# Joined PSUM pairs, whole float32 second products and half tiles in a gated attention plus feed-forward kernel

## The chip, the cores and the metric

One core of a Trainium2 chip (trn2) runs the kernel. The metric is the device time of one execution in microseconds (us). The kernel before took 519.96 us, the median of three runs (518.54 to 520.96).

## The reference

The input is four batches of eight heads, 768 tokens each, head size 48, all float32. The attention is a gated recurrence; its output is the input of a feed-forward layer (FF) with 2048 hidden units.

```python
f = 1.0 / (1.0 + np.exp(-f_logit))
for t in range(S):
    state = f[:, :, t, :, None] * state + einsum('bhd,bhde', k[:, :, t], v[:, :, t])
    y[:, :, t] = einsum('bhd,bhde->bhe', q[:, :, t], state)
x = y.transpose(0, 2, 1, 3).reshape(B * S, H * D)     # 3072 x 384
h = x @ w_in                                           # 384 x 2048
out = (h * np.clip(h + 3.0, 0.0, 6.0) / 6.0) @ w_out   # 2048 x 384
```

## The kernel before

**Attention.** The tokens are cut into chunks of 128 (six per batch), and a chunk of one batch with all its heads is a unit: 24 units, 0 to 23, with the batches of one chunk next to each other. For a unit, VectorE scans the gates backward (`back`, L313), inverts the end values (`rend`, L329 and L330), scans forward (`fwd`, L333), and multiplies keys and queries by the scans (`kmul` L326, `qmul` L339, on VectorE or GpSimd). TensorE transposes the keys (`tk` L400, copied by ScalarE at L407), forms the new state from keys and values (`kv` L419), the scores within the chunk (`att` L378), the part from the carried state (`qs` L451) and the part from the masked scores (`av` L465). The results leave PSUM, TensorE's accumulator memory of eight banks, like this: scores by two masking multiplications, one per bank (`mask0`, `mask1`, L388); states by pairs of additions (`carry0` L432, `carry1` L440, or copies on ScalarE in the first chunk); the output y as a rounded high part on ScalarE (`xh0`, `xh1` L496, `y3h` L482) and the rest on VectorE (`xl0`, `xl1` L502, `y3l` L485). Two DMAs then move rows into the gaps of the FF input (`hole` L508).

**Weights.** The weights arrive as 64-bit words, one tile of 128 hidden units at a time (`ld` L228). ScalarE and VectorE turn each tile into float32 and split it into a high and a low part (L234 to L271; `low` L271 is the last step). There are 16 tiles.

**FF.** Four units make a group of 512 tokens; six groups by 16 hidden tiles give 96 FF tiles. A tile is a first product (`mm1` L528, nine matmuls of 128x512: high by high, high by low, low by high, over three parts of the input), the activation (`relu` L538 on ScalarE, `g` L542 on VectorE), a split of its result (`gh` L547 on ScalarE, `gl` L551 on VectorE), and a second product (`mm2` L565, nine matmuls again, since both sides come in two parts). In the last group a third of the second product runs in halves of 256 tokens (L577).

**Order.** The order of every step is written out in the list ORDER; ON_POOL names the steps that run on GpSimd. Each engine runs its own steps in that order. The digits behind a TensorE step name its PSUM banks. `warm` steps are matmuls on zeros (L660) that fill waits at the start. All loads and stores are issued by SyncE (SP), in order.

```python
P3 = ((0, 0), (0, 1), (1, 0))        # mm1: first index the weight's part, second the input's
a, b = P3[-i]                        # mm2: high by high, low weight by high, high weight by low
```

## Time and profile before

| what | value |
|---|---|
| median of 3 runs | 519.96 us |
| span of the profiled execution, first to last instruction | 519.0 us |
| TensorE matmuls busy | 499.7 us, 96% |
| VectorE busy | 316.3 us, 61% |
| ScalarE busy | 215.5 us, 42% |
| GpSimd busy | 55.5 us, 11% |
| mean granted TensorE clock | 0.987 of full speed |
| bytes moved by DMA | 41.97 MB |

The profile is one execution taken by the hardware profiler; its times count from the span's start. PE is TensorE's matmul side and PEld its weight loads, DVE is VectorE, ACT ScalarE, POOL GpSimd, SP SyncE. A matmul's end is modelled, so the starts of successive groups are the better measure of its pace. The profiled execution took 519.0 us between its first and last instruction, 0.96 us less than the median of the runs.

### The profile page before, as it was taken

Reading aid. Unit: us, or ns where it says so; the run is one execution under the profiler, and the core shown is the slowest. Engines: PE = TensorE matmul, PEld = TensorE weight load, DVE = VectorE, ACT = ScalarE, POOL = GpSimd, SP = SyncE. Lnnn points to the kernel's source line nnn. Section 1 sums busy time; section 2 is a strip of 40 time slices with the busy share of each in tenths; the row PEclk is TensorE's granted clock in tenths of the full one; section 3 lists DMA queues with packets and bytes.
Section 4 is the critical chain, followed back from the end, with each engine's and each line's share of the span. In section 5 each row is a group of like instructions: output and inputs, shape, how many; then the busy total and the mean of one; then the engine's idle time right before and its main releaser. Section 6 shows DMA issues by size and latency. Waiting matters only on the chain.

```text
span 519.0 us, 11607 instructions
## 1 busy us (share of the span) xinstructions
PE 499.7 (96%) x4931; PEld 391.9 (76%) x4931; DVE 316.3 (61%) x599; ACT 215.5 (42%) x390; POOL 55.5 (11%) x61
## 2 busy tenths in 40 slices
...
GB/s 240 242 259 204 140 134 165 255 125 42 80 1 123 53 65 92 97 0 25 98 70 16 115 77 58 39 52 35 64 105 11 12 1 8 62 1 2 0 1 66
DMA packets 24554, 41.97 MB, mean 81 GB/s; under 512 B 2480, under 2 KB 17072, under 8 KB 24496
## 3 DMA queue, kind: packets, MB, share of 16 engines
...
q8 instruction: 41, 0.67, 0.6%
...
## 4 chain that ended last, share of the span: by engine, by line
PE 82%; DVE 8%; ACT 4%; issue 3%; DMA 1%; SPq 0%; POOL 0%; DVEq 0%; ACTq 0%; POOLq 0%
PE h L528 36%; PE o L565 33%; PE y L465 3%; PE o_half L577 2%; PE y L451 2%; PE at L378 2%; PE tk L400 2%; PE kv L419 2%; DVE raw L263 1%; DMA raw<-w 1%; PE idle L660 1%; ACT top L243 1%; ACT weight L268 1%; DVE gg L551 1%; DVE top L259 1%
## 5 line engine op out<-in xcount | busy, mean ns | idle before, releaser
L528 PE MATMUL h<-xt,weight 128*128 128x512 f32 x864 | 220.5, 401 | 2.2 <-ACT raw L234 1.2
L565 PE MATMUL o<-gg,weight 128*128 128x512 f32 x816 | 208.7, 399 | 0.3 <-ACT gg L547 0.3
L528 PEld LDWEIGHTS h<-xt,weight 128*128 128x128 f32 x864 | 160.8, 190 | 40.7 <-ACT top L243 1.3
L565 PEld LDWEIGHTS o<-gg,weight 128*128 128x128 f32 x816 | 151.4, 188 | 36.8 <-DVE gg L551 0.4
L542 DVE SCALAR_TENSOR_TENSOR tg<-tg,h 128x512 f32<-128x512 f32 x96 | 65.9, 686 | 123.7 <-ACT tg L538 123.3
L538 ACT ACTIVATE tg<-h,half 128x512 f32<-128x512 f32 x96 | 66.1, 688 | 178.7 <-PE h L528 176.9
L551 DVE TENSOR_TENSOR gg<-tg,gg 128x512 fp32r<-128x512 f32 x94 | 65.9, 701 | 40.9 <-ACT gg L547 36.9
L547 ACT ACTIVATE gg<-tg 128x512 fp32r<-128x512 f32 x96 | 60.6, 632 | 58.2 <-DVE tg L542 57.4
L326 POOL TENSOR_TENSOR qkf<-qkf,suffix 112x512 f32<-112x512 f32 x17 | 23.2, 1363 | 249.1 <-DVE tg L542 96.1
L313 DVE TENSOR_TENSOR_SCAN suffix<-gates,unit 112x516 f32<-112x516 f32 x24 | 30.3, 1261 | 3.0 <-ACT gates L307 2.8
L333 DVE TENSOR_TENSOR_SCAN suffix<-gates,rend 112x516 f32<-112x516 f32 x24 | 30.1, 1253 | 0.8 <-POOL qkf L326 0.5
L339 POOL TENSOR_TENSOR qkf<-qkf,suffix 112x512 f32<-112x512 f32 x15 | 18.0, 1202 | 42.9 <-DVE suffix L333 39.2
L388 DVE TENSOR_TENSOR a<-at,causal 128x256 f32<-128x256 f32 x48 | 18.1, 416 | 7.3 <-PE at L378 7.1
L465 PEld LDWEIGHTS y<-a,v 64*48 64x48 f32 (+1 forms) x768 | 13.4, 124 | 10.8 <-issue 6.2
L407 ACT ACTIVATE ktok<-tk 128x448 f32<-128x448 f32 (+1 forms) x24 | 12.3, 512 | 19.5 <-PE tk L400 19.4
L465 PE MATMUL y<-a,v 64*48 64x64 f32 (+1 forms) x768 | 17.5, 225 | 2.1 <-DVE a L388 2.0
L263 DVE SCALAR_TENSOR_TENSOR raw<-top,raw 128x768 int16<-128x768 int16 x16 | 18.2, 1138 | 0.5
L378 PE MATMUL at<-qkf 48*64 48x64 f32 x768 | 17.1, 227 | 1.4 <-ACT state L438 1.4
L660 PE MATMUL idle<-blank 128*128 128x512 bf16 x58 | 17.2, 445 | 1.1 <-DVE blank L198 1.1
L268 ACT ACTIVATE weight<-raw 128x768 fp32r<-128x768 f32 x16 | 13.5, 845 | 10.8 <-DVE raw L263 10.8
L496 ACT ACTIVATE xt<-y 112x128 fp32r<-112x128 f32 (+1 forms) x48 | 14.0, 327 | 9.1 <-PE y L465 9.1
L419 PE MATMUL kv<-v,ktok 64*48 64x48 f32 (+1 forms) x768 | 16.2, 216 | 1.6 <-ACT ktok L407 1.4
...
## 6 DMA issues: line engine op xcount, KB each, us to landing
...
gates<-fg SPq DMA_DIRECT2D x24, 226.2 KB, 2.9
...
```

The source lines that it names most:

```text
L263: nc.vector.scalar_tensor_tensor(upper, conv[f]["y"], 8.0, upper, op0=ALU.mult, op1=ALU.add)
L313: nc.vector.tensor_tensor_scan(flat(sf)[:, ::-1], gt[:, 1:][:, ::-1], flat(unit)[:, ::-1], 0.0, op0=ALU.mult, op1=ALU.add,)
L333: nc.vector.tensor_tensor_scan(flat(sf), gt[:, :NP * (C + 1)], flat(rend), 0.0, op0=ALU.mult, op1=ALU.add,)
L378: nc.tensor.matmul(d["ps"][e][HC * odd:HC * (odd + 1), 2 * n + c], t[rs, 1, n, c, odd], t[rs, 0, n, c, odd], start=True, stop=True,)
L419: nc.tensor.matmul(d["kv"][odd][r:r + m, c, n], d["ktok"][rs, 2 * n + part, r:r + m], heads_of(vt[rs], part, n, e)[:, :D], start=(odd, e) ...
L465: nc.tensor.matmul(d["y"][odd][to:to + m, n, cs], heads_of(vt[rs], c, n, e)[:, :m], d["a"][rs, 2 * n + c, e], start=False, stop=True, skip ...
L528: nc.tensor.matmul(h, win[:, f, a, k * 128:(k + 1) * 128], g["xt"][:, k, :g["n"] // C, b], start=i == 0, stop=i == 3 * KT - 1,)
L538: nc.scalar.activation(d["t"], d["h"], AF.Relu, bias=half, scale=1.0 / 6.0)
L542: nc.vector.scalar_tensor_tensor(d["t"], d["t"], 1.0, d["h"], op0=ALU.min, op1=ALU.mult)
L547: nc.scalar.activation(d["gg"][:, 0], d["t"], AF.Copy)
L551: engine("gl", f if g["name"] == "0" else NU).tensor_tensor(d["gg"][:, 1], d["t"], d["gg"][:, 0].bitcast(F32), op=ALU.subtract)
L565: nc.tensor.matmul(g["o"][m], wout[:, f, a, m * 128:(m + 1) * 128], g[f]["gg"][:, b], start=f == 0 and i == 0, stop=f == NF - 1 and i == 2 ...
```

## The change

1. PSUM is now held as two pairs of banks and one single bank. Scores, new states and outputs of a unit lie in one pair, and leave it in one instruction: one `mask`, one `carry0`, one `carry1`, one `xh`, one `xl`. The rows that `hole` moves become a fourth slab of the FF input. States and outputs of neighbouring units share a pair (outputs in columns 0 to 255 of each bank, states from 256 on). Ahead of `av`, TensorE waits on a semaphore until the matmuls of `qs` are done.
2. The second product of the first eight tiles is made of three whole float32 matmuls (`mm2x`, and `mm2a`, `mm2b` for halves). Those tiles need no `gh` and `gl`. A DMA (`wd`) copies the output half of the weight tile in whole float32 to the place of its low part; the low part is made there later (`lowo`), and that of the input half on its own (`lowi`).
3. The first five tiles run in halves of 256 tokens (`mm1a`, `relua`, `ga`, `mm2a` and the same with b), so that the first half needs units 0 and 1 only.
4. Raw weights have two buffers and not three, with two more for the float32 words.
5. ORDER and ON_POOL are new.

```diff
 ON_POOL = """
-kmul.1 qmul.1 kmul.3 qmul.3 kmul.4 qmul.4 kmul.5 gl.0 decay.5 low.3 kmul.6 decay.6 low.9 kmul.7 decay.7 qmul.7
...
+qmul.0 qmul.1 kmul.3 decay.4 qmul.5 kmul.6 decay.6 kmul.7 decay.7 qmul.9 qmul.10 decay.10 qmul.11 decay.11 qmul.12
...
+decay.19 qmul.20 decay.20 qmul.21 kmul.22 qmul.22 kmul.23 qmul.23 lowi.1 lowi.2 lowo.3 lowi.4 lowi.5 lowo.5 lowo.7
...
 ORDER = """
-load.0 loadq.0 load.1 loadv.0 loadq.1 loadv.2 loadv.1 gate.0 loadq.2 back.0 rend.0 kmul.0 gate.1 fwd.0 warm.13
...
+load.0 loadq.0 loadv.0 loadv.1 load.1 loadq.1 loadv.2 gate.0 ld.0 loadq.2 back.0 ld.1 rend.0 kmul.0 warm.16 tk.0.4
...
+    pairs = [ps_g.tile([128, 2, 512], F32, name=f"pair{i}") for i in range(2)]
+    single = ps_g.tile([128, 512], F32, name="single")
...
+    def conv_keep(f):
+        nc.sync.dma_start(out=weight[:, f, 1, OUTS].bitcast(F32), in_=conv[f]["w"][:, OUTS])
...
+        "low": lambda f: conv_low("low", f, slice(0, WN), conv[f]["w"]),
+        "lowi": lambda f: conv_low("lowi", f, INS, conv[f]["w"][:, INS]),
+        "lowo": lambda f: conv_low("lowo", f, OUTS, weight[:, f, 1, OUTS].bitcast(F32)),
...
-            d["ps"] = [bank([128, NP, HC], f"at{i}_{e}") for e in range(2)]
+            d["at"] = pair()[:, :, :NP * HC].rearrange("r e (p t) -> r e p t", t=HC)
...
+        def mask():
+            d["a"] = sb.tile([128, NP, 2, HC], F32, tag="a", name=f"a{i}")
+            nc.vector.tensor_tensor(
+                d["a"].rearrange("r p e t -> r e p t"), d["at"],
+                causal.unsqueeze(1).unsqueeze(1).broadcast_to([128, 2, NP, HC]), op=ALU.mult,
+            )
...
-            d["kv"] = [bank([128, 2, 2, D], f"kv{i}_{odd}") for odd in range(2)]
+            d["kv"] = pair()[:, :, 256:256 + 4 * D].rearrange("r o (c n d) -> r o c n d", c=2, n=2)
...
-            d["y"] = [bank([128, 2, C], f"y{i}_{odd}") for odd in range(2)]
+            d["y"] = pair()[:, :, :2 * C].rearrange("r o (n t) -> r o n t", t=C)
...
+            d["qs"] = nc.cur_bb.bb.instructions[-1]
...
         def av():
             vt = values[i]
+            hold = nc.tensor.nop()
+            after(hold.ins, d["qs"], mybir.DependencyClass.Sync)
...
+        def xh():
+            nc.scalar.activation(parts(0), d["y"][:PR], AF.Copy)
+        def xl():
+            nc.vector.tensor_tensor(parts(1), d["y"][:PR], parts(0).bitcast(F32), op=ALU.subtract)
...
+    def mm2_whole(g, f):
+        outs_of(g, f)
+        for m in range(KT):
+            nc.tensor.matmul(
+                g["o"][m], wout[:, f, 1, m * 128:(m + 1) * 128].bitcast(F32), g[f]["t"],
+                start=f == 0, stop=f == NF - 1, skip_group_check=True,
+            )
+    def half_of(p):
...
+        def mm2(g, f):
+            outs_of(g, f + p)
+            for m in range(KT):
+                nc.tensor.matmul(
+                    g["o"][m][:, p * 256:(p + 1) * 256],
+                    wout[:, f, 1, m * 128:(m + 1) * 128].bitcast(F32), g[f, p]["t"],
+                    start=f + p == 0, stop=False, skip_group_check=True,
+                )
```

How the order moves shows at three places. The names in the rows are the tiles written and read, with their unit or FF tile; L numbers are lines of the version that the rows belong to.

**VectorE at units 1 and 2, the first weight tile.** Before, the scores are masked and the outputs split by several instructions each, and the first weight tile (`raw0`, `top0`) comes behind unit 3's scans:

```order
L388 TENSOR_TENSOR a1_344<-at1_0_310,causal_80 128x4x64
L388 TENSOR_TENSOR a1_344<-at1_1_311,causal_80 128x4x64
L313 SCALAR_TENSOR_TENSOR suffix1_74<-gates1_73,unit_90 112x516
L329 TENSOR_SCALAR ends_111<-suffix1_74 112x4
L330 RECIPROCAL rend_109<-ends_111 112x4
L485 TENSOR_TENSOR y3_1_401<-y1_1_299,y3_1_401 112x128
L502 TENSOR_TENSOR xt0_248<-y1_1_299,xt0_248 112x128
L333 SCALAR_TENSOR_TENSOR suffix1_74<-gates1_73,rend_109 112x516
L247 TENSOR_SCALAR raw0_308<-top0_405 128x768
L502 TENSOR_TENSOR xt0_248<-y1_0_298,xt0_248 112x2x128
```

With the change, one instruction each does unit 1's mask and split, and the weight tile comes ahead of unit 2's scan:

```order
L240 TENSOR_SCALAR raw0_127<-top0_252 128x768
L392 TENSOR_TENSOR a1_305<-pair0_70,causal_83 128x2x4x64
L246 TENSOR_SCALAR top0_252<-top0_252 128x768
L252 TENSOR_TENSOR top0_252<-top0_252,raw0_127 128x768
L256 SCALAR_TENSOR_TENSOR w0_283<-top0_252,w0_283 128x768
L493 TENSOR_TENSOR xts_111<-pair1_71,xts_111 112x2x2x128
L320 SCALAR_TENSOR_TENSOR suffix0_75<-gates0_74,unit_93 112x516
```

The weight work moved ahead of two scans, and five instructions of unit 1 became two.

**TensorE behind unit 2, and SyncE's queue there.** Before, the first FF product stands behind unit 4's `av`. With the change the first half of tile 0 (`th0_0`, `single` of 256 columns) stands between unit 2's `qs` and `av`:

```order
L454 MATMUL pair0_70<-qkf2_129,middle0_96 64x64 x8
L575 MATMUL single_72<-xts_111,weight_73 128x256 x9
L471 MATMUL pair0_70<-a2_449,v2_124 64x64 x8
L471 MATMUL pair0_70<-a2_449,v2_124 48x64 x8
L404 MATMUL pair1_71<-ident_78,qkf3_215 128x112 x4
L593 MATMUL o0_0_482<-th0_0_454,weight_73 128x256
```

In SyncE's queue the copies of whole weights (`weight<-w0`, `weight<-w1`) stand between the loads:

```order
L310 DMA v4_338<-v 128x400
L498 DMA xts_111<-xts_111 16x3x256 x2
L272 DMA weight_73<-w0_283 128x384
L222 DMA raw2_351<-w 128x3072
L301 DMA gates0_74<-fg 112x517
L222 DMA raw3_428<-w 128x3072
L305 DMA qkf5_447<-qk 112x1024
L310 DMA v5_480<-v 128x400
L301 DMA gates1_76<-fg 112x517
```

Two units' work moved from ahead of the first FF product to behind it, and each copy is a step that the loads behind it are issued after.

**TensorE at units 14 and 15.** Before, the attention products stand in several stretches between FF products:

```order
L451 MATMUL y14_0_2984<-qkf14_2357,decayed2_104 64x64 x2
...
L378 MATMUL at14_1_3003<-qkf14_2357 64x64
L565 MATMUL o2_0_2590<-gg2_9_2967,weight_70 128x512
...
L528 MATMUL h2_11_3042<-xt2_1915,weight_70 128x512 x9
...
L400 MATMUL tk15_3071<-ident_75,qkf15_2870 128x112 x4
L528 MATMUL h2_12_3076<-xt2_1915,weight_70 128x512 x9
L465 MATMUL y14_0_2984<-a14_3034,v14_2425 48x64 x2
...
L419 MATMUL kv15_0_3110<-v15_2920,ktok15_3086 64x48
```

With the change `qs`, the next unit's `att`, `av` and the next unit's `kv` follow each other:

```order
L454 MATMUL pair0_70<-qkf14_2149,decayed0_98 64x64 x8
L454 MATMUL pair0_70<-qkf14_2149,middle0_96 64x64 x8
L385 MATMUL pair1_71<-qkf15_2452 64x64 x16
L471 MATMUL pair0_70<-a14_2574,v14_2181 48x64 x16
L423 MATMUL pair0_70<-v15_2489,ktok15_2633 64x48
...
L517 MATMUL single_72<-xts_111,weight_73 128x512 x9
```

Three stretches of attention work between FF products became one, and the transposes of units 15 and 16 stand together elsewhere.

## Rows read from the trace of the kernel before

**Rows 1.** Two stretches: us, busy us (count) of PE, PEld, DVE, ACT, POOL, clock, DMA.

```profile
91.00:104.00 13.00, 11.91 (x110) 8.87 (x108) 12.63 (x21) 8.04 (x11) 2.93 (x3) 1.00 0.77 254
460.00:500.00 40.00, 40.00 (x200) 33.44 (x199) 13.58 (x22) 11.90 (x18) 0.00 (x0) 1.00 0.00 1
```

**Rows 2.** The chain that ended last, in order of time: start us, us, what.

```profile
110.64 1.86 issue
112.50 0.78 PE tk L400 x4
113.28 3.46 PE h L528 x9
...
124.31 4.22 PE h L528 x18
128.53 2.10 PE o L565 x9
```

**Rows 3.** The same chain at its end.

```profile
510.60 2.15 PE o_half L577 x18
```

**Rows 4.** VectorE's timeline: start us, us, engine, line, operation, out and in.

```profile
124.58 0.96 DVE L271 TENSOR_TENSOR weight<-raw,weight 128x768 fp32r<-128x768 f32 x1
```

**Rows 5.** Groups of VectorE instructions: count, busy us, mean ns, idle before and its releasers.

```profile
L542 DVE SCALAR_TENSOR_TENSOR tg<-tg,h 128x512 f32<-128x512 f32 x96 | 65.9, 686 | 123.7 <-ACT tg L538 123.3
L551 DVE TENSOR_TENSOR gg<-tg,gg 128x512 fp32r<-128x512 f32 x94 | 65.9, 701 | 40.9 <-ACT gg L547 36.9 <-PE o_half L577 2.1 <-PE o L565 1.4
L388 DVE TENSOR_TENSOR a<-at,causal 128x256 f32<-128x256 f32 x48 | 18.1, 416 | 7.3 <-PE at L378 7.1
L502 DVE TENSOR_TENSOR xt<-y,xt 112x256 fp32r<-112x256 f32 x24 | 10.0, 418 | 0.0
L502 DVE TENSOR_TENSOR xt<-y,xt 112x128 fp32r<-112x128 f32 x24 | 6.9, 287 | 1.2 <-ACT y L482 0.8 <-ACT xt L496 0.3
L432 DVE TENSOR_TENSOR middle<-kv,decayed 112x96 f32<-112x96 f32 x40 | 8.3, 251 | 3.4 <-PE kv L419 3.3
L271 DVE TENSOR_TENSOR weight<-raw,weight 128x768 fp32r<-128x768 f32 x14 | 14.9, 1067 | 1.2 <-ACT weight L268 0.9
L313 DVE TENSOR_TENSOR_SCAN suffix<-gates,unit 112x516 f32<-112x516 f32 x24 | 30.3, 1261 | 3.0 <-ACT gates L307 2.8
L326 DVE TENSOR_TENSOR qkf<-qkf,suffix 112x512 f32<-112x512 f32 x7 | 5.3, 761 | 4.9 <-DMA qkf<-qk 4.8
```

**Rows 6.** TensorE's timeline at unit 2's carried-state product and at the first FF product.

```profile
28.45 0.58 PE L451 MATMUL y<-qkf,middle 48*64 48x64 f32 x14 [0.44 <-ACT middle L430]
...
43.63 1.19 PE L528 MATMUL h<-xt,weight 128*128 128x512 f32 x4
```

**Rows 7.** TensorE's timeline around units 8 to 10, between FF products.

```profile
154.85 0.60 PE L400 MATMUL tk<-ident,qkf 112*128 112x112 f32 x4
155.46 2.35 PE L528 MATMUL h<-xt,weight 128*128 128x512 f32 x9
157.74 0.67 PE L465 MATMUL y<-a,v 64*48 64x64 f32 x32
158.22 0.63 PE L419 MATMUL kv<-v,ktok 64*64 64x48 f32 x32
158.79 2.37 PE L565 MATMUL o<-gg,weight 128*128 128x512 f32 x9
161.00 0.55 PE L400 MATMUL tk<-ident,qkf 112*128 112x112 f32 x4
161.31 2.34 PE L528 MATMUL h<-xt,weight 128*128 128x512 f32 x9
163.59 0.46 PE L451 MATMUL y<-qkf,decayed 48*64 48x64 f32 x16
```

**Rows 8.** Weight loads of the FF products: count, busy us, mean ns, idle before.

```profile
L528 PEld LDWEIGHTS h<-xt,weight 128*128 128x128 f32 x864 | 160.8, 190 | 40.7 <-ACT top L243 1.3 <-ACT ktok L407 0.8 <-DVE a L388 0.6
```

**Rows 9.** A kind of DMA: count, KB each, median us from issue to landing.

```profile
gates<-fg SPq DMA_DIRECT2D x24, 226.2 KB, 2.9
```

More of the change, by code (lines that the diff above doesn't have):

```diff
@@ new lines @@
+wd.0 ld.2 high.0 mid.1 kmul.2 rend.2 warm.12 tk.2.4 lowi.0 gate.3 fwd.2 ktok.2 warm.2 kv.2.0 lim.1 load.4 qmul.2
+carry0.2 dif.1 att.2.2 carry1.2 back.3 ld.3 qs.2.0 mm1a.0.4 loadq.5 mask.2 kmul.3 rend.3 relua.0 av.2 ga.0 fwd.3
+tk.3.2 xh.2 loadv.5 mm2a.0 ktok.3 z.2 xl.2 load.5 qmul.3 kv.3.2 gate.4 hole.2 top.1 att.3.0 carry0.3 carry1.3 mask.3
+cy.2 wd.1 qs.3.2 loadq.6 back.4 av.3 high.1 loadv.6 xh.3 mid.2 kmul.4 xl.3 lowi.1 tk.4.4 mm1a.1.0 rend.4 hole.3 ktok.4
+lim.2 fwd.4 gate.5 kv.4.2 relua.1 z.3 dif.2 ga.1 decay.4 ld.4 load.6 mm2a.1 top.2 back.5 cy.3 wd.2 mm1b.0.4 high.2
@@ new lines @@
+mid.3 kmul.5 mm1b.1.1 relub.0 lim.3 gb.0 lowi.2 tk.5.0 rend.5 relub.1 mm2b.0 carry0.4 ktok.5 dif.3 decay.5 ld.5
+mm1a.2.4 gb.1 gate.6 fwd.5 z.4 mm1b.2.0 top.3 relua.2 mm2b.1 relub.2 ga.2 qmul.5 wd.3 cy.4 gb.2 load.7 carry1.4 mm2b.2
+high.3 mid.4 qmul.4 lim.4 mm2a.2 lowi.3 dif.4 z.5 back.6 mm1a.3.4 ld.6 gate.7 mm1b.3.1 top.4 relua.3 ga.3 kmul.6
+high.4 wd.4 att.4.2 rend.6 mm2a.3 mask.4 relub.3 cy.5 lowi.4 gb.3 mm1a.4.4 mid.5 fwd.6 mm2b.3 relua.4 lim.5 load.8 z.6
+ga.4 dif.5 tk.6.0 mm2a.4 qmul.6 ld.7 ktok.6 top.5 mm1b.4.4 back.7 cy.6 wd.5 qs.4.0 relub.4 mid.6 gate.8 gb.4 kv.5.2
@@ new lines @@
+decay.6 loadq.7 av.4 high.5 rend.7 lim.6 kv.6.0 loadv.7 carry0.5 lowi.5 mm1.5.4 carry0.6 carry1.5 xh.4 dif.6 carry1.6
+lowo.3 ld.8 z.7 xl.4 mm2b.4 relu.5 top.6 g.5 kmul.7 cy.7 wd.6 att.5.2 hole.4 att.6.0 mask.5 high.6 mm2x.5 mid.7 lowo.4
+lim.7 lowi.6 dif.7 fwd.7 ld.9 mm1.6.4 z.8 top.7 qmul.7 cy.8 wd.7 tk.7.2 load.9 lowo.0 ktok.7 mid.8 relu.6 lowo.1 lim.8
+high.7 g.6 qs.5.2 av.5 decay.7 kv.7.2 dif.8 mm2x.6 lowi.7 xh.5 ld.10 top.8 loadv.8 z.9 loadq.8 gate.9 xl.5 lowo.5 cy.9
+mask.6 hole.5 mm1.7.4 high.8 lowo.6 mid.9 carry0.7 lim.9 low.8 mm1.8.0 relu.7 dif.9 z.10 lowo.2 ld.11 top.9 relu.8 g.7
@@ new lines @@
+cy.10 carry1.7 mm2x.7 g.8 high.9 mid.10 back.8 gh.8 lim.10 gl.8 qs.6.0 att.7.2 dif.10 av.6 low.9 ld.12 mm2.8 xh.6
+loadv.9 top.10 loadq.9 z.11 mask.7 lowo.7 cy.11 xl.6 mm1.9.4 high.10 mid.11 hole.6 kmul.8 lim.11 low.10 mm1.10.2
+relu.9 dif.11 z.12 g.9 ld.13 top.11 gh.9 qs.7.0 relu.10 gl.9 av.7 cy.12 g.10 mm2.9 loadv.10 high.11 mid.12 loadq.10
+rend.8 gh.10 lim.12 low.11 xh.7 mm1.11.4 dif.12 gl.10 z.13 ld.14 top.12 mm2.10 relu.11 fwd.8 cy.13 g.11 load.10
+high.12 mid.13 tk.8.3 qmul.8 gh.11 ktok.8 lim.13 low.12 mm1.12.4 dif.13 z.14 gl.11 ld.15 mm2.11 gate.10 top.13 relu.12
@@ new lines @@
+tk.15.4 relu.36 tk.16.1 mm1.37.2 ktok.15 gl.35 ktok.16 g.36 gate.17 fwd.16 gh.36 mm2.35 relu.37 back.17 load.18 g.37
+mm1.38.4 rend.17 gh.37 gl.36 gl.37 gate.18 qmul.16 mm2.36 relu.38 back.18 g.38 mm2.37 gh.38 gl.38 mm2.38 mm1.39.4
+mm1.40.3 relu.39 g.39 gh.39 mm1.41.4 relu.40 gl.39 g.40 gh.40 mm2.39 relu.41 gl.40 g.41 gh.41 mm2.40 gl.41 mm2.41
+qs.14.0 att.15.2 decay.16 loadq.17 av.14 kv.15.0 mask.15 loadv.17 mm1.42.4 xh.14 xl.14 carry0.15 hole.14 carry1.15
+mm1.43.2 relu.42 kmul.17 g.42 gh.42 fwd.17 mm1.44.4 relu.43 gl.42 load.19 g.43 qmul.17 mm2.42 rend.18 gh.43 relu.44
```

346 lines of the change are left out of this document (149 added, 197 removed).

## The prediction, made before the changed kernel ran

> **What bounds the kernel now.** I read the tenths in 40 slices first, then busy times by stretch, then the chain of waits in order of time, and TensorE's and VectorE's timelines where the chain changes hands. Two stages are to be seen. In 91 to 104 us VectorE is busy 12.63 of 13 us; in 460 to 500 us TensorE is busy all 40 us [rows 1]. The chain shows where the first stage gives way: at 110.64 TensorE idles 1.86 us, then needs 3.46 us for nine matmuls of a first product that take 2.11 us later (4.22 for 18), and from there the chain is TensorE's alone [rows 2]. I cut the run at the end of FF tile 15's first product, the last that needs a new weight: 128.53 us [rows 2]. From there to the end of the last half product, 510.60 + 2.15 = 512.75 us [rows 3], are 384.2 us of TensorE; the rest of the span, 519.0 - 512.75 = 6.25 us, is the last copy, store and close. The sum is 128.53 + 384.22 + 6.25 = 519.0, the profiled execution; the median of the runs stands 0.96 us above.
>
> **Stage 1, VectorE.** The last weight part (`low.15`) starts at 124.58 and takes 0.96 us, so it ends at 125.54 [rows 4]; TensorE reached tile 15 some 3 us later, held up by the slow stretch at 110 to 117 us [rows 2]. I count VectorE's instructions up to `low.15` in both orders.
> Gone: 6 `g` at 0.686 and 6 `gl` at 0.701 (8.3 us); 16 masks at 18.1/48 = 0.377 (6.0); the three parts of `xl` for 8 units at 0.418 + 0.287 + 0.287 (7.9; the smallest, L485, has the 128-column shape); 8 pairs of carries at 2 x 8.3/40 = 0.415 (3.3); 6 whole `low` at 1.067 (6.4). Together 31.9 us [rows 5].
> Added: 10 half `g` of 256 columns, which I take at the mask's 0.42 (4.2); 9 masks of 512 columns and 8 `xl` of 512. No row has these, so they are bounded from below by 0.418 (256 columns) and from above by two such (0.84); the step from 128 to 256 columns costs 0.131, so 512 cost about 0.418 + 2 x 0.131 = 0.68, near the 0.686 of `g`, which reads as many from PSUM (17 x 0.67 = 11.4). 10 joined carries between 0.25 and 0.415, taken as 0.33 (3.3). 4 `lowi` and 5 `lowo` of half width, 1.067/2 = 0.53 (4.8). New on VectorE, since GpSimd has fewer of them: 4 `kmul` at 0.761 and 2 `qmul`, taken as the same (4.6). One more `back` and one more `fwd` at 1.26 (2.5), one `decay` at about 0.4. Together 31.2 us [rows 5].
> So VectorE's work up to `low.15` is 0.7 us less: the joins and the missing `gl` pay for what came over from GpSimd and for unit 8, which is now done earlier. I take VectorE's waits as they were, and `low.15` ends at 125.54 - 0.7 = 124.8. Only the last three of a first product's nine matmuls use the low weight, so tile 15 ends 0.7 us behind it: **125.5 us**, if TensorE is there. ScalarE (8.04 of 13 us busy) and GpSimd (2.93) have room in that stage [rows 1]: ScalarE loses six `gh` and two of three copies per unit, GpSimd has 16 steps up to the cut and not 18. The eight `wd` copies and what they hold up in SyncE's queue I cost at nothing, since the loads run ahead of their use; that cover is a rival below.
>
> **Stage 1, TensorE.** It must now do more: by the cut, one first product less (-2.1; tile 16 follows the cut), unit 8's `qs`, `att` and `av` more (about 0.5 + 0.6 + 0.5 = 1.6), and whole float32 second products. Of these no row exists. `av` has 16 float32 products of 64 columns and shows 32 matmuls: two per product. They take 158.22 - 157.74 = 0.48 us [rows 7], in four corners of the array at once, so each takes 4 x 0.48/32 = 60 ns; at 512 columns 0.48 us, two per product 0.96, three products 2.88 us per tile, against 2.11 now. The lower end is one pass each as now, 3 x 0.234 = 0.70. I take 2.88, the nearest in kind: 8 x 0.77 = 6.2 us more. The Trainium skill's page "FP8 and Floating Point Precision", section "TensorE Precision Notes", states that true FP32 takes four passes through the array; by it a tile is 4 x 3 x 0.234 = 2.81 us, an estimate, and the eight cost 5.6 us more in place of 6.2. The two matmuls per product are what the trace shows of it. Halves as such cost nothing: 18 half matmuls take 2.15 us, 0.119 each, half of 0.234 [rows 3].
> TensorE thus has 5.7 us more to do, but starts earlier. The first FF product began at 43.63; now it follows unit 2's `qs`, which ran at 28.45 [rows 6]. That is 15.2 us, so TensorE could be at the cut at 128.53 + 5.7 - 15.2 = 119.0. VectorE's 125.5 counts: a gain of 3.0 us, and the float32 price is hidden behind VectorE by 6.5 us. If that cover goes, 6.2 us come back in part.
>
> **Stage 2, TensorE.** Behind the cut the work changes by +2.1 - 1.6 = +0.5 us. What falls away is changing over. A tile between attention stretches takes 157.74 - 155.46 = 2.28 or 161.00 - 158.79 = 2.21 us [rows 7] against 2.11 undisturbed, so entering and leaving a stretch costs about 0.2 us together. I count the stretches of attention work behind the cut: 40 before, 8 of them transposes alone; now 23, 6 of them transposes alone. The 32 others become 17: 15 x 0.2 = 3.0 us. A transpose group directly behind other attention work takes 155.46 - 154.85 = 0.61, one behind an FF product 161.31 - 161.00 = 0.31 [rows 7]; there are 4 of the dear kind before and 3 now: 0.3 us. The new wait of `av` for `qs` costs nothing where the next unit's `att` (163.59 less 0.5 for `qs`, about 0.6 us) stands between them, as in nearly all stretches; without that cover I bound it by the change-over, 0.2 us each. Together 384.2 + 0.5 - 3.3 = 381.4.
>
> **Sum.** 125.5 + 381.4 + 6.25 = 513.1 us for a profiled execution, 514.0 for a median.
>
> **The rivals.**
> *TensorE is late again, or the wait is dear.* The early stage has more to do on two engines that are both nearly full, and 3 us of it hang on no stall like that at 110.64. If tile 15 ends at 128.5 as before, only stage 2's 2.8 us remain: 517.1. If besides each of 24 holds costs 0.1 us: 519.5. For it speaks that the slow stretch sits just where VectorE and TensorE meet; against it the 15 us of earlier start. No change, or nearly.
> *SyncE's queue: slower.* Each of eight `wd` copies waits for VectorE's join of that weight tile, and the loads behind it are issued only then; gates that arrive late stop VectorE's scans, on which everything hangs in stage 1. A fully exposed load of gates is 2.9 us [rows 9]; eight are 23 us, 537; four 525.6. It decides from three on (8.7 us, 522.7). Against it: at the first copies the loads for the next two units are already issued ahead.
> *Whole float32 loads its weights in the open.* The FF products' loads, 190 ns each, hide behind matmuls of 234 ns [rows 8]. Five half tiles with 12 matmuls and three whole ones with 6 make 78 loads; all in the open cost 14.8 us, TensorE reaches the cut at 133.8 and not 125.5: 522.3. Against it: 60 ns per matmul in `av` include its loads. The Trainium skill's page "TensorE: Matmul & The Clock Gate", section "Weight-path perf modes — Fast Weight Load (FWL) and DoubleRow", states that the fast load is off for FP32 input, which is the rule that speaks against this part; the trace before has no float32 load of 128 columns beside a 512-column product, and does not show it.
> *The joins are cheaper than taken.* If the 17 joined instructions cost the lower bound, 0.42 and not 0.67, VectorE is done 4.3 us earlier, and the cut comes at 121.2, still behind TensorE's 119.0: 509.8 us. For it speaks nothing in the rows; the stretch at 91 to 104 us, with 0.37 us idle in 13 [rows 1], says that each us saved there counts.
>
> **Chances.** Forecast 0.55; late or dear wait 0.20; SyncE's queue 0.10; loads in the open 0.05; cheaper joins 0.10. A measurement tells 0.5%, 2.6 us, from no change: faster means below 517.4, slower above 522.6. Faster: the last and most of the first, and the near end of the second: 0.68. Slower: the queue and the far part of the loads: 0.11. The rest, 0.21, is no change. The range takes in the cheaper joins and, 2 us below them, change-overs at 0.3 us each (15 x 0.1 more), and reaches past the dear wait and most of the way to the open loads: 508 to 521.
>
> **What would show it.** Right: VectorE's last weight subtraction ends near 125 us, the first FF product starts near 28, `mask` and `xl` read 0.65 to 0.7 us, a whole float32 matmul of 512 columns starts every 0.43 to 0.48 us, stretches of about 2.1 us with `qs`, `att`, `av`, `kv` and no gap, and TensorE needs about 381 us from tile 15's first product to its end. Wrong: idle VectorE scans released by gate loads, TensorE idle or at half clock before 125 us, gaps ahead of `av`.

## Result and the profile after

The changed kernel takes **513.18 us** (median of 4 runs, 512.35 to 514.08) against 519.76 us (4 runs, 518.54 to 520.96) for the kernel before: ratio 0.987, 95% interval 0.985 to 0.989. Forecast were 514.0 us, 508 to 521. The profiled execution took 512.78 us, its span 511.1.

With the prediction's cut (end of FF tile 15's first product) and the end of the last half product, all profiled executions split like this (us; stage 2 is the difference of the first two columns, the tail is span less the second; e1 to e12 are the experiments below):

| kernel | cut | end of TensorE | stage 2 | span | median |
|---|---|---|---|---|---|
| before | 128.53 | 512.75 | 384.2 | 519.0 | 519.76 |
| forecast | 125.5 | 506.9 | 381.4 | 513.1 | 514.0 |
| after | 119.72 | 505.39 | 385.7 | 511.1 | 513.18 |
| e1 other banks in the last group | 119.04 | 502.94 | 383.9 | 508.6 | 510.56 |
| e2 conversion steps together | 128.78 | 513.74 | 385.0 | 519.4 | 521.84 |
| e3 joins split | 119.40 | 505.07 | 385.7 | 510.6 | 513.68 |
| e4 two first products twice | 125.78 | 512.18 | 386.4 | 517.7 | 517.66 |
| e5 split second products | 135.00 | 520.85 | 385.9 | 527.0 | 526.97 |
| e6 no halves | 127.47 | 514.92 | 387.5 | 520.6 | 521.95 |
| e7 av behind qs | 120.34 | 507.60 | 387.3 | 513.1 | 514.80 |
| e8 stretches split | 120.38 | 517.49 | 397.1 | 523.0 | 524.77 |
| e9 waits mended | 119.34 | 501.63 | 382.3 | 507.9 | 510.77 |
| e10 stage 1 filled | 122.08 | 503.99 | 381.9 | 510.2 | 513.73 |
| e12 kv apart | 119.26 | 506.83 | 387.6 | 512.6 | 514.33 |

One reading has to be evened out first. The cut of the kernel before is the recorded end of tile 15's first product, as in the prediction; the other rows of measured kernels take the start of the product behind it, which in the kernel before is at 128.37. Like for like, stage 1 gained 8.6 us and stage 2 lost 1.3 us. So the total was met, but not by its parts: 3.0 us were forecast to be gained in stage 1, and 2.8 us in stage 2. Executions with the changed kernel's own order in stage 2 (after, e2 to e6) read 385.0 to 387.5 there; a difference below 2 us in that column needs a local reading beside it.

**Where the cut lies now.** TensorE's timeline of the changed kernel at tiles 15 and 16 (start, length, engine, line, shape; L517 is the first product, L471 `av`) answers to [rows 2]:

```profile
116.92 0.67 PE L471 MATMUL pair<-a,v 64*48 64x64 f32 x32
117.52 2.37 PE L517 MATMUL pair<-xts,weight 128*128 128x512 f32 x9
119.72 2.26 PE L517 MATMUL single<-xts,weight 128*128 128x512 f32 x9
```

Tile 15 is the second row; tile 16 follows at 119.72 without a gap, and the idle, slow stretch of [rows 2] has no counterpart. The last weight subtraction, which answers to [rows 4], in VectorE's timeline:

```profile
117.04 0.94 DVE L264 TENSOR_TENSOR weight<-w,weight 128x768 fp32r<-128x768 f32 x1
```

It ends at 117.98, while the three matmuls of tile 15 that read it start at 117.52 + 6 x 0.234 = 118.92. VectorE is 0.9 us ahead, so at tile 15 TensorE is held by its own queue and not by VectorE. Further ahead VectorE does hold it: of the 6.9 us that TensorE waits between 20 us and the cut, 5.5 are for results of VectorE.

**VectorE's sum.** The windows view up to the end of that subtraction (length, then busy time and instructions of PE, PEld, DVE, ACT, POOL, granted clock, DMA share, GB/s), before and after:

```profile
0.00:125.54 125.54, 112.74 (x1417) 81.18 (x1418) 112.97 (x207) 77.59 (x139) 26.02 (x35) 0.96 0.61 185
```

```profile
0.00:117.98 117.98, 106.92 (x1538) 79.66 (x1539) 105.87 (x188) 71.85 (x112) 22.08 (x31) 0.99 0.69 216
```

VectorE's busy time (third pair) fell by 7.1 us; 0.7 were forecast. The sizes of single joined instructions were near, as the groups of the changed kernel show (busy us, mean ns; compare [rows 5]):

```profile
L392 DVE TENSOR_TENSOR a<-pair,causal 128x512 f32<-128x512 f32 x24 | 16.4, 683 | 28.3 <-PE pair L471 26.1 <-PE pair L385 2.2
L493 DVE TENSOR_TENSOR xts<-pair,xts 112x512 fp32r<-112x512 f32 x24 | 16.4, 683 | 3.3 <-ACT xts L490 3.2
L438 DVE TENSOR_TENSOR middle<-pair,decayed 112x192 f32<-112x192 f32 x20 | 6.9, 347 | 0.9 <-ACT xts L490 0.5 <-PE pair L423 0.3
```

The joined mask and low part of y take 0.683 us (taken: 0.67), the joined carry 0.347 (0.33). Busy time is the time in which at least one instruction is recorded, so it can differ from the sum of their durations. Up to the last weight subtraction, that sum is 123.0 us before and 118.4 after: 4.6 us of the 7.1 are in the durations, and 2.5 in how far instructions overlap. VectorE's timeline of the kernel before, the first three of the four conversion steps of one tile:

```profile
94.72 0.35 DVE L247 TENSOR_SCALAR raw<-top 128x768 int16<-128x768 int16 x1
95.10 0.36 DVE L253 TENSOR_SCALAR top<-top 128x768 int16<-128x768 int16 x1
95.49 0.56 DVE L259 TENSOR_TENSOR top<-top,raw 128x768 int16<-128x768 int16 x1
```

and of the changed kernel, where the same steps (now L240, L246, L252) alternate with others:

```profile
89.22 0.36 DVE L240 TENSOR_SCALAR raw<-top 128x768 int16<-128x768 int16 x1
89.49 0.69 DVE L333 TENSOR_TENSOR qkf<-qkf,suffix 112x512 f32<-112x512 f32 x1
90.09 0.35 DVE L246 TENSOR_SCALAR top<-top 128x768 int16<-128x768 int16 x1
90.36 0.95 DVE L264 TENSOR_TENSOR weight<-w,weight 128x768 fp32r<-128x768 f32 x1
91.23 0.55 DVE L252 TENSOR_TENSOR top<-top,raw 128x768 int16<-128x768 int16 x1
```

Before, each step begins 0.03 us behind the recorded end of the one that it depends on (94.72 + 0.35 = 95.07, next 95.10). After, an independent neighbour begins 0.08 to 0.09 us ahead of it (89.22 + 0.36 = 89.58, next 89.49). That is 0.12 us a neighbour, and a sum of durations doesn't see it.

The durations fell for another reason as well. Some VectorE instructions take up to 1.5 us longer than the median of their kind. Each one that is over 0.15 us longer, in the traces of the kernel before, the changed kernel and e2 alike, overlaps an instruction of GpSimd (one such pair stands at e2). Up to the last weight subtraction the time above the median adds up to 5.9 us before and 4.0 after: 1.9 us of the 4.6. No run moved GpSimd's steps by themselves.

On the overlap of neighbours, the Trainium skill's page "Perfetto Trace Analysis", section "Optimizing Scalar/DVE Operations", says that part of a profiled instruction overlaps with the next one; the trace agrees for independent neighbours, by 0.08 to 0.09 us, and shows that dependent ones have none of it.

**Whole float32 second products**, in TensorE's timeline of the changed kernel (L565 on 512 columns, L593 on 256):

```profile
46.54 4.05 PE L593 MATMUL o<-th,weight 128*128 128x256 f32 x18
50.24 1.42 PE L575 MATMUL single<-xts,weight 128*128 128x256 f32 x9
...
66.56 2.84 PE L565 MATMUL o<-tg,weight 128*128 128x512 f32 x6
68.84 2.66 PE L517 MATMUL single<-xts,weight 128*128 128x512 f32 x9
```

A whole tile takes 68.84 - 66.56 = 2.28 us, 0.38 a matmul (0.48 forecast), three half tiles 3.70, so 1.23 each. Against 2.11 and 9 x 0.119 = 1.07 the eight tiles cost 3 x 0.17 + 10 x 0.16 = 2.1 us more, not 6.2. By the Trainium skill's page "FP8 and Floating Point Precision", section "TensorE Precision Notes", with its four passes for true FP32, an estimate from 0.234 us a pass would be 0.47 a matmul; the trace differs, and decides.

**Stage 2.** TensorE's waits from 122 us on in the changed kernel; the same view of the kernel before has one of 0.2 us:

```profile
PE pair L423 <- issue: 0.7, 1, 0.7
PE pair L517 <- DVE state L445: 0.6, 1, 0.6
PE o L557 <- ACT gg L536: 0.6, 1, 0.6
PE pair L404 <- POOL qkf L346: 0.4, 1, 0.4
PE single L517 <- DVE tg L531: 0.4, 1, 0.4
```

There is also a stall that this view doesn't list, in the last group (TensorE's timeline; L608 is the half product):

```profile
459.55 2.25 PE L517 MATMUL pair<-xts,weight 128*128 128x512 f32 x9
461.63 1.56 PE L557 MATMUL o<-gg,weight 128*128 128x512 f32 x6
463.30 0.98 PE L608 MATMUL pair<-gg,weight 128*128 128x256 f32 x6
464.11 2.26 PE L517 MATMUL single<-xts,weight 128*128 128x512 f32 x9
466.21 1.57 PE L557 MATMUL o<-gg,weight 128*128 128x512 f32 x6
467.62 0.88 PE L608 MATMUL pair<-gg,weight 128*128 128x256 f32 x6
```

A tile's half products begin 1.41 us behind its other second products (467.62 - 466.21), but 1.67 where the first product ahead of them wrote bank 0 (463.30 - 461.63), and take 0.81 to the next start instead of 0.72: 0.35 us lost, at five tiles, 1.7 us.

### The profile page after: what moved, and what is told of

The parts are those of the page before. It is cut to its first block, busy times and chain, and to the rows that moved or that the text cites. A ratio compares the mean times of both kernels' runs of the same rounds, so it can differ in the third digit from the quotient of the medians.

```text
span 511.1 us, 11476 instructions
## 1 busy us (share of the span) xinstructions
PE 490.8 (96%) x4960; PEld 388.7 (76%) x4960; DVE 302.1 (59%) x496; ACT 207.1 (41%) x331; POOL 50.6 (10%) x59
## 4 chain that ended last, share of the span: by engine, by line
PE 51%; DMA 1%; DVE 1%; ACT 1%; issue 0%; POOL 0%; ACTq 0%
PE o L557 22%; PE pair L517 12%; PE single L517 11%; PE pair L608 3%; PE pair L454 1%; PE pair L471 1%; DMA qkf<-qk 1%; ACT tg L527 1%; PE pair L385 1%; DVE tg L531 1%; PE pair L423 1%; DMA outT<-os 1%; PE single L404 0%; PE pair L404 0%; DVE os L618 0%
## 5 line engine op out<-in xcount | busy, mean ns | idle before, releaser
L557 PE MATMUL o<-gg,weight 128*128 128x512 f32 x744 | 183.9, 398 | 0.6 <-ACT gg L536 0.6
L517 PE MATMUL single<-xts,weight 128*128 128x512 f32 x423 | 108.2, 400 | 0.5 <-DVE tg L531 0.4
L517 PE MATMUL pair<-xts,weight 128*128 128x512 f32 x396 | 99.5, 396 | 0.6 <-DVE state L445 0.6
L517 PEld LDWEIGHTS single<-xts,weight 128*128 128x128 f32 x423 | 78.1, 188 | 20.4 <-DVE tg L531 1.2
L517 PEld LDWEIGHTS pair<-xts,weight 128*128 128x128 f32 x396 | 73.5, 188 | 17.9 <-DVE state L445 1.0
L531 DVE SCALAR_TENSOR_TENSOR tg<-tg,single 128x512 f32<-128x512 f32 x47 | 32.1, 683 | 50.5 <-ACT tg L527 50.4
L527 ACT ACTIVATE tg<-single,half 128x512 f32<-128x512 f32 x47 | 32.3, 687 | 65.6 <-PE single L517 63.5
L531 DVE SCALAR_TENSOR_TENSOR tg<-tg,pair 128x512 f32<-128x512 f32 x44 | 30.0, 683 | 34.5 <-ACT tg L527 30.3
L527 ACT ACTIVATE tg<-pair,half 128x512 f32<-128x512 f32 x44 | 30.1, 687 | 35.3 <-PE pair L517 30.8
L346 POOL TENSOR_TENSOR qkf<-qkf,suffix 112x512 f32<-112x512 f32 x16 | 21.5, 1345 | 88.1 <-DVE suffix L340 84.0
```

What stands on the lines that cost most here:

```text
L346: engine("qmul", i).tensor_tensor(parts_of(t, 0), parts_of(t, 0), split(sf[:, :, 1:]), op=ALU.mult)
L517: nc.tensor.matmul(h, win[:, f, a, k * 128:(k + 1) * 128], g["xt"][:, k, :g["n"] // C, b], start=i == 0, stop=i == 3 * KT - 1,)
L527: nc.scalar.activation(d["t"], d["h"], AF.Relu, bias=half, scale=1.0 / 6.0)
L531: nc.vector.scalar_tensor_tensor(d["t"], d["t"], 1.0, d["h"], op0=ALU.min, op1=ALU.mult)
L557: nc.tensor.matmul(g["o"][m], wout[:, f, a, m * 128:(m + 1) * 128], g[f]["gg"][:, b], start=f == 0 and i == 0, stop=f == NF - 1 and i == 2 ...
```

## Experiments

All are edits of the changed kernel except e11; `...` marks what is left out of an edit. Medians are compared with 513.18; ratios are against the kernel before in the same round.

**e1: the last group's banks.** Part of the edit (bank numbers in the order):

```
-mm1.80.3 ... mm1.81.0 ... mm2p.80.1 ... mm2q.80.2 ... mm1.82.4 ... mm1.83.3
+mm1.80.0 ... mm1.81.4 ... mm2p.80.2 ... mm2q.80.3 ... mm1.82.0 ... mm1.83.4
```

> The changed kernel with other banks in the last group (FF tiles 80 to 95): both half outputs lie in one pair of banks, first products take the other pair and the single bank by turns. Theory: in the changed kernel a half product that writes one bank of a pair waits for VectorE's read of the other bank, since the pair is one tile; five half products start 0.34 us late for that (1.7 us in all). Then they read 0.72 us like the others, the tile period there is 4.2 us, and the time falls by 1.7 us, to about 511.5 us (profiled execution 509.4). Rival: those half products wait because VectorE and ScalarE are late in the last group, whatever the banks; then the late starts stay and the time is 513.2 us.

510.56 us (ratio 0.985, 0.982 to 0.989), with stage 2 1.8 us shorter. The late starts are gone in its timeline:

```profile
457.80 2.26 PE L517 MATMUL pair<-xts,weight 128*128 128x512 f32 x9
459.90 1.56 PE L557 MATMUL o<-gg,weight 128*128 128x512 f32 x6
461.30 0.88 PE L608 MATMUL pair<-gg,weight 128*128 128x256 f32 x6
462.02 2.25 PE L517 MATMUL single<-xts,weight 128*128 128x512 f32 x9
```

The half products start 1.40 us behind, also where the pair was written. The stall came from a pair being one tile: a write of one bank waits for VectorE's read of the other. One new wait of the same kind came: the last two half products now wait 0.52 us for the copy of the first half output.

**e2: VectorE's conversion steps put together** (tiles 3 to 15; tile 8 shown, only VectorE's steps):

```
-mid.8 lowo.1 lim.8 g.6 dif.8 lowi.7 top.8
+lowo.1 g.6 lowi.7 mid.8 lim.8 dif.8 top.8
```

> The changed kernel with VectorE's four conversion steps of weight tiles 3 to 15 put one behind the other, as before the change; the same instructions, only VectorE's order differs. Theory A: what VectorE gained up to its last weight subtraction beyond the forecast (7.6 us against 0.7) came from the order: a step next to the one that it depends on starts about 0.05 us after that one's recorded end, an independent one about 0.09 us ahead of it. 39 such neighbours at about 0.13 us are 5 us; VectorE was 0.9 us ahead of TensorE at tile 15, so the cut comes some 4 us later: about 517 us. Rival: the gain came from shorter single instructions and the joins, the order of the conversion is indifferent: 513.2 us, within 0.5.

521.84 us (ratio 1.005, 1.003 to 1.007): the whole gain is gone by the order of the same instructions. Its windows row up to the last weight subtraction:

```profile
0.00:127.55 127.55, 108.53 (x1540) 80.51 (x1541) 111.79 (x188) 71.74 (x112) 19.93 (x31) 0.97 0.63 200
```

VectorE's busy time rises from 105.87 to 111.79 us with the same 188 instructions (5 us expected). About half of the 5.9 us, 3.1, is overlap between neighbours that is gone. The other 2.8 are longer durations, which the expectation did not have: four of the moved second conversion steps now run beside an instruction of GpSimd and take 1.04 to 1.35 us. One of them, from the timelines of VectorE and GpSimd:

```profile
93.43 1.04 DVE L246 TENSOR_SCALAR top<-top 128x768 int16<-128x768 int16 x1
92.70 1.56 POOL L264 TENSOR_TENSOR weight<-weight 128x384 fp32r<-128x384 f32 x1 [12.23 <-PE o L565]
```

In the changed kernel none of the 16 steps of this kind takes more than 0.36 us. TensorE receives results later and waits 10.0 us for VectorE ahead of the cut instead of 5.5; the cut moves by 9.1 us and not by 4. The order of VectorE's instructions is shown to carry the gain; how much of it goes by neighbours and how much by GpSimd is read from the traces only.

**e3: joins split**

```
-nc.vector.tensor_tensor(parts(1), d["y"][:PR], parts(0)..., op=ALU.subtract)
+for o in range(2):
+    nc.vector.tensor_tensor(parts(1)[:, o], d["y"][:PR, o], parts(0)[:, o]..., op=ALU.subtract)
```

and `mask` and the carries likewise.

> The changed kernel with VectorE's joined exits split again, each into two instructions on one bank each: mask, the low part of y, both carries. Nothing else changes. The prediction's sizes (0.67 us joined against 2 x 0.416, and 0.33 against 2 x 0.25 for carries) give 17 x 0.16 + 10 x 0.17 = 4.4 us more on VectorE up to the last weight subtraction, less the 0.9 us that VectorE is ahead of TensorE there: 516.7 us. Rival: by start to start, as a queued instruction begins 0.08 us ahead of the recorded end of the last, two halves cost 2 x 0.335 = 0.67 and the joined one 0.60: 17 x 0.07 + 10 x 0.08 = 2.0 us more, less 0.9: about 514.3 us. If the joins give nothing: 513.2 us.

513.68 us (ratio 0.989, 0.987 to 0.992), cut at 119.40: no loss that shows. VectorE's busy time to its last subtraction is 107.24 us, 1.4 more, with 27 instructions more. Their recorded durations add up to 4.0 us more, near the 4.4 of the forecast's sizes, but most of that overlaps. The joins by themselves are worth next to nothing in time here.

**e4: two first products issued twice**

```
+for again in range(2 if g["name"] == "0" and f in (6, 9) else 1):
```

> The changed kernel with the first products of FF tiles 6 and 9 issued twice (the second pass writes the same values again): 4.2 us more on TensorE before the cut, nothing more on any other engine. The prediction's statement that VectorE sets the cut at tile 15 and that TensorE has some us of room behind it: the time stays at 513.2 us, at most 514. Rival: with float32 second products at 0.17 us dearer per tile instead of 0.77 and VectorE faster than forecast, TensorE itself sets the cut now (it idles only 2.3 of the 79.7 us from 40 us to the cut, VectorE is done 0.9 us ahead): nearly all of the 4.2 us shows, about 517 us.

517.66 us (ratio 0.997, 0.995 to 0.999; 515.19 to 520.36): the 4.2 us show in full. The cut in the table moved by 6.1 us, because TensorE was already 2.0 us late at tile 6 in this execution. From tile 6 on, where the first of the two doubled products stands, its timeline reads

```profile
70.80 4.76 PE L518 MATMUL single<-xts,weight 128*128 128x512 f32 x18
```

and from there to the cut are 125.78 - 70.80 = 54.98 us, against 119.72 - 68.84 = 50.88 in the changed kernel: 4.1 us more. In the windows view VectorE is as busy as before the edit and only waits longer:

```profile
0.00:124.06 124.06, 113.76 (x1556) 84.98 (x1557) 105.67 (x188) 72.05 (x112) 22.14 (x31) 0.96 0.67 205
```

The statement that VectorE sets the cut and TensorE has room is false for the changed kernel. That does not make VectorE free: e2 changes VectorE's order alone and moves the cut further.

**e5: second products split again** (tokens of tile 0's first half and of tile 5):

```
-wd.0 ... lowi.0 ... ga.0 ... mm2a.0 ... g.5 ... mm2x.5
+lowi.0 lowo.0 ... ga.0 gha.0 ... gla.0 mm2a.0 ... g.5 gh.5 ... gl.5 mm2.5
```

> The changed kernel with the eight whole float32 second products undone: each takes the high and low parts again (9 matmuls, high part on ScalarE, low part on VectorE), the output half of the low weights comes straight from the converted tile behind its input half, and the copies of whole weights are gone. On VectorE 10 subtractions of 256 columns and 3 of 512 come back, start to start 10 x 0.33 + 3 x 0.63 = 5.2 us; TensorE loses 8 x 0.17 = 1.4 us. Theory: what the float32 products buy is VectorE's time; without them VectorE sets the cut, 5.2 - 0.9 us later: about 517.5 us. Rival: TensorE sets the cut and the float32 products are only dearer there: 511.8 us.

526.97 us (ratio 1.013, 1.009 to 1.016), more than either theory. TensorE waits 6.8 us for the high parts of halves and 3.7 us for those of whole tiles, and its granted clock reads 0.86, 0.93 and 0.78 in the three stretches of 12 us from 38 us on, where the changed kernel has 1.00. The two steps lengthen the way from gate to second product in an order that leaves no room for them. What the float32 products give is the shorter way as well as VectorE's time; this run doesn't part the two.

**e6: no halves** (tile 0 shown)

```
-mm1a.0.4 relua.0 ga.0 mm2a.0 ... mm1b.0.4 relub.0 gb.0 mm2b.0
+mm1.0.4 relu.0 g.0 mm2x.0
```

> The changed kernel with FF tiles 0 to 4 whole: one first product of 512 columns in the place of the second half's, the same order otherwise. Two half tiles (first and second products, 4.3 us of TensorE) then no longer run ahead of 37 us; VectorE loses five instructions, about 0.3 us. Theory: TensorE sets the cut now and its early start counts: about 517 us. Rival, the prediction's order of things: VectorE sets the cut, TensorE has room: 513 us.

521.95 us (ratio 1.003, 1.0003 to 1.005): 8.8 us more where about 4 were expected. Windows of this run and of the changed kernel:

```profile
26.00:38.00 12.00, 7.58 (x216) 6.35 (x216) 11.34 (x18) 5.68 (x11) 3.01 (x3) 0.63 0.94 269
38.00:50.00 12.00, 10.68 (x62) 7.70 (x61) 8.18 (x16) 6.21 (x10) 1.91 (x2) 0.66 0.51 164
```

```profile
26.00:38.00 12.00, 9.49 (x268) 7.84 (x260) 11.93 (x19) 7.11 (x14) 2.99 (x3) 1.00 0.85 248
38.00:50.00 12.00, 10.91 (x73) 10.03 (x70) 11.63 (x25) 7.91 (x13) 3.15 (x2) 1.00 0.65 207
```

Without the early halves TensorE is busy 7.58 instead of 9.49 of 12 us, and its granted clock is 0.63 and 0.66 over these 24 us where the changed kernel has 1.00. So part of the 7.8 us at the cut is work that comes later, and part goes with the clock; the shares are not shown. Nor do the early halves always come with the full clock: e1 and e9, which have the changed kernel's order in stage 1, read 0.81 to 0.91 between 32 and 44 us, and e6 reads 0.50 there, the lower of the two levels (1.2 GHz).

**e7: av directly behind qs**

```
-qs.9.0 att.10.2 ... av.9 kv.10.0
+qs.9.0 av.9 att.10.2 ... kv.10.0
```

> The changed kernel with av put directly behind qs of the same unit in seven attention stretches of stage 2, where the next unit's att stood between them, so that nothing covers av's wait for the end of qs. The prediction: the wait is hidden by att, and bounded by 0.2 us each without it: 7 x 0.2 = 1.4 us at most, 514.6 us, and each qs to av shows a gap. Rival: the wait costs nothing either way, TensorE's queue ends qs before av could start: 513.2 us and no gap; or it is dearer than bounded, 0.4 us each: 516 us.

514.80 us (ratio 0.990, 0.987 to 0.993). The hold is seen in TensorE's timeline:

```profile
157.62 0.41 PE L454 MATMUL pair<-qkf,middle 48*64 48x64 f32 x16
158.13 0.66 PE L471 MATMUL pair<-a,v 64*48 64x64 f32 x32
158.61 0.65 PE L385 MATMUL pair<-qkf 48*64 48x64 f32 x32
```

`av` starts 0.51 us behind the last group of `qs`. In the changed kernel `att` starts 0.23 behind it, and `av` costs nothing:

```profile
157.00 0.41 PE L454 MATMUL pair<-qkf,middle 48*64 48x64 f32 x16
157.23 0.65 PE L385 MATMUL pair<-qkf 48*64 48x64 f32 x32
```

That is 0.28 us each, and 2.0 us for seven; the median rose by 1.6. The prediction's cover is real, and its bound of 0.2 is a little low.

**e8: stretches split by an FF product**

```
-qs.9.0 att.10.2 ... av.9 kv.10.0 ... mm1.23.4
+qs.9.0 att.10.2 ... mm1.23.4 av.9 kv.10.0 ...
```

> The changed kernel with an FF product moved between att and av in the same seven stretches of stage 2, so that each becomes two; no work is added. The prediction: entering and leaving a stretch costs 0.2 us: 7 x 0.2 = 1.4 us more, 514.6 us. Rival: the change-over costs nothing by itself (the longer FF product beside a stretch only overlaps its neighbour in the records), and stage 2's gain came from elsewhere: 513.2 us.

524.77 us (ratio 1.009, 1.006 to 1.012): the run can't decide. TensorE's waits in stage 2 are 10.6 us, mostly for carries, masks and a copy of y that now come late. The two places that can be read, one without a wait and one with a listed wait of 0.36 us taken off, show 0.35 and 0.31 us more; a mean over all seven says nothing about changing over.

**e12: kv apart**, the better test:

```
-qs.9.0 att.10.2 ... av.9 kv.10.0 ... mm1.23.4 xh.9 xl.9
+qs.9.0 att.10.2 ... av.9 ... mm1.23.4 xh.9 xl.9 kv.10.0
```

> The changed kernel with kv of four attention stretches of stage 2 (with units 9, 10, 14 and 15) moved behind the FF product that followed the stretch, so that kv stands alone between two FF products; nothing that soon needs its result is delayed, unlike in the run that split seven stretches. The prediction: one more entering and leaving costs 0.2 us; from one stretch's qs to the end of the FF product behind kv TensorE then takes 0.2 us longer at each of the four places, 0.8 us in all: 514.0 us. Rival: 0.33 us each, as the two undisturbed places of the run with seven stretches split read (0.31 and 0.35): 1.3 us, 514.5 us. If changing over costs nothing: no longer, 513.2 us.

514.33 us (ratio 0.991, 0.988 to 0.995). TensorE's timeline with unit 10:

```profile
171.62 0.46 PE L454 MATMUL pair<-qkf,decayed 48*64 48x64 f32 x16
...
173.16 2.37 PE L557 MATMUL o<-gg,weight 128*128 128x512 f32 x9
175.46 0.67 PE L423 MATMUL pair<-v,ktok 64*64 64x48 f32 x32
176.06 2.36 PE L557 MATMUL o<-gg,weight 128*128 128x512 f32 x9
178.35 0.46 PE L454 MATMUL pair<-qkf,decayed 48*64 48x64 f32 x16
```

The changed kernel has the same two `qs` here:

```profile
171.50 0.46 PE L454 MATMUL pair<-qkf,decayed 48*64 48x64 f32 x16
177.88 0.46 PE L454 MATMUL pair<-qkf,decayed 48*64 48x64 f32 x16
```

From one to the next are 178.35 - 171.62 = 6.73 us in this run and 177.88 - 171.50 = 6.38 in the changed kernel for the same work: 0.35 us for one more stretch. The place with unit 9 gives 0.35 as well. So a change-over costs 0.35 and not 0.2.

**e9: four waits of stage 2 mended**, on top of e1:

```
-mm1.19.4 ... mm1.20.0 ... mm2.16      mm1.51.4 mm1.52.0   mm2.79 outv.13 outs.12 ... relu.80 g.80 gh.80 gl.80
+mm1.19.4 ... mm2.16 mm1.20.0 ...      mm1.51.0 mm1.52.4   relu.80 g.80 gh.80 gl.80 mm2.79 outv.13 outs.12 ...
-mm2q.93 outh.15 mm2q.94 odh.15 mm2q.95 outh.16 odh.16
+mm2q.93 mm2q.94 mm2q.95 outh.15 outh.16 odh.15 odh.16
```

> The banks of the last group as in the run with other banks there, and besides, by moves in the order alone: the copy of the first half output behind the last half product (a half product waited 0.52 us for it, since both halves now lie in one pair), the second product of tile 16 ahead of the first product of tile 20 (0.6 us of waiting for the carries' read of a pair), banks of tiles 51 and 52 exchanged (0.35), the gate of tile 80 ahead of the copies of group 4's outputs on ScalarE and VectorE (0.57). Theory: stage 2 lost what its fewer change-overs gave to such waits of TensorE; then these four, 2.0 us, go and the time is about 508.5 us. Rival: a mended wait comes back as one of the next instruction (TensorE's inputs are late as such): 510.6 us as with the banks alone.

510.77 us (ratio 0.983, 0.979 to 0.987; 509.36 to 514.27). Stage 2 fell to 382.3 us, 1.6 below e1, but the tail grew from 5.7 to 6.3, since both half outputs are now copied at the end. In the time it is not to be told from e1. Both medians lie below the changed kernel's, but the intervals of the ratios overlap; what shows that the waits are gone is stage 2.

**e10: stage 1 filled**, on top of e9:

```
-tk.4.4 mm1a.1.0 ...      mm2a.1 ... mm1b.0.4
+mm1a.1.0 tk.4.4 ...      mm1b.0.4 mm2a.1 ...
```

> The kernel of the waits mended, and in stage 1 the first half product of tile 1 put ahead of unit 4's transposes, for which TensorE waits 2.1 us at 33.7 us, and the first half product of tile 0's second half ahead of the second product of tile 1, for which it waits 1.1 us at 38.1. No work is added or removed. Theory: TensorE sets the cut in the changed kernel, so idle time of TensorE that is filled in stage 1, up to 2 us, comes off the end: about 507 us. Rival: VectorE sets the cut, or what is filled here waits later for VectorE: 508.5 us, as with the waits mended.

513.73 us (ratio 0.987, 0.984 to 0.990): 3.0 us slower than e9. TensorE's timeline there:

```profile
39.92 2.26 PE L575 MATMUL single<-xts,weight 128*128 128x256 f32 x9 [2.46 <-DMA xts<-xts]
41.98 2.76 PE L593 MATMUL o<-th,weight 128*128 128x256 f32 x6
```

The half product of tile 0's second half was ready only when a copy of y landed at 39.9 us, and nothing could pass it. The windows view gives a granted clock of 0.55 from 40 to 46 us; 9 half matmuls take 2.06 us there and not 1.1. The attempt failed, but it shows again that a delay of TensorE (2.7 us at the cut against e9) goes through to the end.

**e11: the kernel before with its conversion steps parted** (tile 8 shown):

```
-tk.6.4 gl.6 ld.10 z.8 mask0.5 decay.6 mm2.6 mask1.5 ktok.6 mid.8 lim.8 dif.8 top.8
+tk.6.4 mid.8 gl.6 ld.10 z.8 lim.8 mask0.5 decay.6 mm2.6 dif.8 mask1.5 ktok.6 top.8
```

> The kernel before the change, with nothing altered but VectorE's order: the conversion steps of weight tiles 3 to 15 are moved ahead by up to three places each, so that an instruction of another kind stands between two steps that depend on each other (35 such neighbours parted). Theory: by the run with these steps put together (39 neighbours, 7.2 us of VectorE's time, 0.18 each) VectorE saves 35 x 0.18 = 6.4 us up to its last weight subtraction; TensorE gets its operands earlier and the cut comes 3 to 6 us earlier: 514 to 517 us, so that the order alone gives about half of what the change gave or more. Rival: in the kernel before TensorE was held by its own late start and slow stretch, 3 us behind VectorE; then VectorE is done earlier and the time stays at 519.8 us.

527.25 us (ratio 1.013, 1.009 to 1.018): slower. The parting did add 2.6 us of overlap, but instructions that run beside one of GpSimd now cost 7.6 us instead of 5.9, so VectorE's busy time to its last subtraction falls only from 112.97 to 110.71 us. It also waits now where it didn't: 3.8 us for ScalarE's `cy` (2.0 before) and 4.1 for its `relu` (0.4 before). Parting alone, by moving steps ahead, doesn't carry the gain over. That the other engines' orders must fit is the likely reason; no run shows it.

## Why the prediction was right, point by point

The total was right by luck: two errors in opposite directions nearly cancelled, 5.6 us of gain too little in stage 1 and 4.1 too much in stage 2; 0.5 us of the tail came on top.

- **VectorE up to the last subtraction, forecast 0.7 us less, end at 124.8: wrong**, 7.1 us less, end at 117.98. The counts were right, and so were the sizes of joined and half instructions, within 0.02 us. Three things failed in the sum. It took the old masks and carries at busy time over count (0.377 and 0.208 us), but the new ones at recorded durations; the old ones' mean durations are 0.416 and 0.251 [rows 5], which makes 1.3 us. It had no term for overlap between neighbours, 2.5 us, and none for instructions that run beside GpSimd's, 1.9 us. Together these are 5.7 of the 6.4 us that it missed. The last two depend on the order: e2 gives back 5.9 of the 7.1 us by nothing but order.
- **VectorE alone sets the cut, and TensorE has 6.5 us of room: wrong.** TensorE has no room (e4, e10), and VectorE's results still delay it ahead of the cut (e2). The forecast put TensorE at 119.0 and it came to 119.72, but by errors that cancel: the float32 products cost 2.1 us and not 6.2, while the remaining attention work of units 2 to 4, formerly ahead of the first FF product, came behind it (the eight pieces from 27.90 to 38.08 us take 5.1 us) and TensorE waited 2.1 and 1.1 us at 33.7 and 38.1. The early start that the forecast counted was real (26.56 us, 28.45 expected), and e6 shows its worth, together with the clock.
- **Joins pay for what came over from GpSimd: not shown.** e3 takes them apart at no loss of time. What the pairs allow besides, one `xh` a unit and a shorter queue on ScalarE, wasn't tried by itself.
- **Stage 2, 3.3 us less from fewer change-overs: the mechanism holds, its price was too low, and the gain was given back.** Like for like, 384.4 + 0.5 (moved work) + 2.5 (waits listed, less the 0.2 of before) + 1.7 (pairs) - 385.7 = 3.4 us are left as gained, which is what was forecast. But this is a remainder, and e12 puts a change-over at 0.35 us, by which 15 would give 5.2; 1.8 us of that were not found. The step that failed is that the forecast had no term for new waits of TensorE: 4.2 us. e1 and e9 together take 3.4 us out of stage 2.
- **The hold costs nothing: right** where `att` stands between (no gap in a joined stretch), and 0.28 us each without it (e7). The changed kernel itself has places without it in stage 1: `av` starts 0.50 us behind the last group of `qs` at 73.66 and 0.51 at 94.13.
- **The tail** was taken as 6.25 us, and it is 5.7.
- **Rivals.** SyncE's queue did not stop VectorE's scans. VectorE waited 4.5 us for gates in three places, 2.8 in one before, but the last of these waits ends at 20.84 us and SyncE issues the first copy of a whole weight only at 21.45. What the copies held up is a step of ScalarE, by 3.2 us at 67 to 70 us. Float32 loads in the open are excluded by a whole tile at 2.28 us. TensorE was not late again: the cut was early. The joins were not cheaper: they cost what was taken, and VectorE was quicker for the reasons above.
